# Spreading maxima by one transpose, and casting high halves on GpSimd, in a packed attention + MLP kernel

## The chip, the cores and the metric

One core of a Trainium2 chip runs the whole program. The metric is device time in microseconds (us) per execution.

## The reference

Inputs: `q`, `k`, `v` of 8 batches x 8 heads x 576 positions x 64, `p` of 8 x 8 x 32 x 64, `w_in` 512 x 2048, `w_out` 2048 x 512 (the kernel handles weights of 8-byte floats).

```python
p_packed = sm_attn(p, k, v)             # 32 packed positions attend to k, v
out = sm_attn(q, p_packed, p_packed)    # every q attends to the 32
x = out.transpose(0, 2, 1, 3).reshape(B * S, H * D)
h = x @ w_in
sp = maximum(h, 0) + log1p(exp(-abs(h)))
return (h * erf(sp)) @ w_out
```

## The kernel before, in words

For each batch b the packed result p_packed is folded into `w_in` (`w_prime`), so that h = a2 @ w', where a2 are the second softmax's weights. Products are made in parts: a high part plus a low remainder. Batches 0 and 1 use fp32r parts; batches 2 to 7 use 16-bit (f16) parts, which need scales that are powers of two, so that nothing leaves f16's range.

The work is cut into 128 **units** (b, c, i): a half c of a batch's 576 positions and a pair i of 128-blocks of d_ff. A unit is 12 matmuls of h (`h_half`, two halves of 6, L598), the gate on ScalarE and VectorE, a split into `gh` and `gl`, and 24 matmuls of o (`o_part`, four parts d, L650), which come some steps later. Units 0 to 31 are batches 0 and 1; their activations are softplus and erf. From unit 32 a form with tanh is used.

The first 20 units stand in an order written out by hand (`BEGINNING`). After them `step(n, outs)` issues unit n's h, then the o parts of earlier units, and between these what the table `plan` holds for `(n, where)`: `do(n, 0)` and `do(n, 1)` behind the first o part, `do(n, 3)` behind the third, `do(n, 2)` at the step's end. `ATTEND` (batches 2 and 3) and `ATTEND_LATER` say in which slots the generator `attention(b)` makes its next piece. Every engine executes in the order of issue; `keep_order` fixes it.

PSUM: `ps_h` has two banks, taken in turn by the halves of h, by single-bank scores and by the small products below; `ps_m` is one tile of two banks, used by `w_prime`, by scores and by the attention's tile `p`; `ps_o` holds the four o sums. SBUF: the ring `wo` (18 tiles) holds the parts of `w_out`, the reloaded pairs `wox` and their halves `woh`.

**The scales.** `tallest_in` and `tallest_out` (L175) take per-partition maxima of `w_in` and `w_out`; `gather` (L195) reduces them to one column. `turn` (L201) transposes this column to one row in a `ps_h` bank, and `two_over` (L187 to L190, three VectorE instructions) makes 2/max of it as one number. `spread` (L209, L211) multiplies that number by a row of ones, which puts it on all 128 partitions, in another `ps_h` bank, and copies it to SBUF. The norm of each batch from 2 on goes the same way: L498 transposes, `two_over` reduces, and `spread_norm` (L219, L221) spreads; here both rows and columns lie in spare columns of the `ps_m` tile `p`, which stays taken until the copy L221.

`out_weights` makes `sigma` from the maximum of `w_out`; `whole(i)` reloads a pair of `w_out`'s blocks from DRAM (SP queue), and `halve(i)` makes the f16 high half on ScalarE (L254) and the low half on VectorE (L255), for i = 0 to 7, in steps 30 to 37:

```python
both = opool.tile([P, 2, 2, DM], F16, name=f"woh{i}", tag="wo")
nc.scalar.mul(both[:, 0], pairs[i][:], sigma[:])
nc.vector.scalar_tensor_tensor(both[:, 1], pairs[i][:], sigma[:], both[:, 0], ...)
```

GpSimd (POOL) makes memsets at the start and issues the output DMAs of batches 0 and 1 (L665, L667).

Of the kernel before, what the change touches and what calls it, by code (L numbers as in the profile page):

```python
# [8 lines left out]
F32 = mybir.dt.float32  # L9
# [6 lines left out]
ALU = mybir.AluOpType  # L16
# [25 lines left out]
K12 S12 W1.3 W1.2 o11.0 o10.1 o11.1 o10.3 h15.0 H1.3 L14 F15 s14 V1.3 H1.2 T12 h15.1 L13 o11.3 p11.1 m12 U12 d15.1 M0 C  # L42
o10.2 o11.2 v12 c15.0 s15 h16.0 p11.2 p11.0 h16.1 c16.1 K14 m13 R14 o12.2 d16.0 s16 K13 S13 u13 v13 p11.3 e14 T13
o12.1 h17.0 h19.0 d19.0 o12.0 m14 e15 V1.2 m15 o12.3 e16 U14 v14 L15 K15 h17.1 c17.1 o13.1 o13.0 h19.1 c17.0 C c19.1
S15 o13.3 o14.1 h18.0 h18.1 m16 O0 O1 s19 s17 d18.0 C C C d18.1 M1 M2 M3 s18 e18 U15 o14.0 m18 e19 v15 e17 o13.2 o14.2 T15 m19 o14.3
# [5 lines left out]
def tile_pack_attention_moe(ctx: ExitStack, tc: tile.TileContext, qT, kT, v, pT, w_in, w_out, outT):  # L51
    nc = tc.nc
    P = 128
    B, _, NC, S = qT.shape
# [37 lines left out]
    ones = cpool.tile([1, P], F32, name="ones")  # L92
# [15 lines left out]
    nc.gpsimd.memset(ones[:], 1.0)  # L108
# [89 lines left out]
    def turn(kind):  # L198

        row = ps_h.tile([P, 512], F32, name=f"row_{kind}", tag="ps_h")  # L200
        nc.tensor.transpose(row[0:1, 0:P], halved[kind][:], ident[:])  # L201
        one = cpool.tile([1, 1], F32, name=f"one_{kind}")
        two_over(one[:], row[0:1, 0:P])
        halved[kind] = one

    def spread(kind):

        row = ps_h.tile([P, 512], F32, name=f"col_{kind}", tag="ps_h")
        nc.tensor.matmul(row[:, 0:1], ones[:], halved[kind][:], start=True, stop=True)  # L209
        inverse[kind] = cpool.tile([P, 1], F32, name=f"inv_{kind}")  # L210
        nc.vector.tensor_copy(inverse[kind][:], row[:, 0:1])  # L211
# [4 lines left out]

    def spread_norm(b, po, one):

        nc.tensor.matmul(po[:, 2 * P:2 * P + 1], ones[:], one[:], start=True, stop=True)  # L219
        inverse[b] = apool.tile([P, 1], F32, name=f"inv{b}", tag="inv")  # L220
        nc.vector.tensor_copy(inverse[b][:], po[:, 2 * P:2 * P + 1])  # L221
# [29 lines left out]
    def halve(i):  # L251

        both = opool.tile([P, 2, 2, DM], F16, name=f"woh{i}", tag="wo")
        nc.scalar.mul(both[:, 0], pairs[i][:], sigma[:])  # L254
        nc.vector.scalar_tensor_tensor(both[:, 1], pairs[i][:], sigma[:], both[:, 0], op0=ALU.mult, op1=ALU.subtract)  # L255
        for k in range(2):
            half_hi[2 * i + k], half_lo[2 * i + k] = both[:, 0, k, :], both[:, 1, k, :]
# [23 lines left out]
    ATTEND_LATER = ((-12, 2), (-6, 0), (-6, 1), (-4, 0), (-4, 1), (-4, 2), (-3, 2), (-2, 3), (-2, 2), (-1, 3), (-1, 2),  # L281
                    (0, 0), (0, 1), (1, 0), (1, 1), (1, 2), (2, 0), (2, 1), (4, 0), (4, 1),
# [44 lines left out]
    def attention(b):  # L327
# [169 lines left out]
        if b >= NB0:  # L497
            nc.tensor.transpose(po[0:1, P:2 * P], norm[:], ident[:])  # L498
# [4 lines left out]
        if b >= NB0:  # L503
            one = apool.tile([1, 1], F32, name=f"one{b}", tag="one")
            two_over(one[:], po[0:1, P:2 * P])
            if not third:
                yield
                spread_norm(b, po, one)
        yield
        ta = apool.tile([P, 2, S], F32, name=f"ta{b}", tag="big", bufs=3)  # L510
        for c2 in range(2):
            banks = bank(f"s2_{c2}", b > NB0 + 1 or (b >= NB0 and c2 == 0) or (b == 1 and c2 == 1))
            for c in range(NC):
                for r in range(2):
# [270 lines left out]
    def slot(n, where):  # L785
        return plan.setdefault((n, where), [])
# [123 lines left out]
```

## Time and profile before

| | |
|---|---|
| time, median of 3 (lowest to highest) | 706.14 us (705.68 to 707.76) |
| the profiled execution | 706.21 us, of which the span is 704.4 us |
| PE busy | 682.3 us, 97% |
| VectorE (DVE) busy | 596.9 us, 85% |
| ScalarE (ACT) busy | 563.1 us, 80% |
| GpSimd (POOL) busy | 44.8 us, 6%, all of it in the first third |
| granted TensorE clock | 0.999 of 2.4 GHz |

Time outside the span (1.8 us) belongs to the start and end of the execution. A line like "PE wp L551 <- DVE inv L221: 2.5, 4, 0.7" says that PE's instructions of line 551 waited 2.5 us in all, 4 times, for VectorE's line 221. In a timeline, the bracket behind an instruction is the idle time before it and what ended it.

### The profile page before, as it was taken

Reading aid. Unit: us, or ns where it says so; the run is one execution under the profiler, and the core shown is the slowest. Engines: PE = TensorE matmul, PEld = TensorE weight load, DVE = VectorE, ACT = ScalarE, POOL = GpSimd, SP = SyncE. Lnnn points to the kernel's source line nnn. Section 1 sums busy time; section 2 is a strip of 40 time slices with the busy share of each in tenths; the row PEclk is TensorE's granted clock in tenths of the full one; section 3 lists DMA queues with packets and bytes.
Section 4 is the critical chain, followed back from the end, with each engine's and each line's share of the span. In section 5 each row is a group of like instructions: output and inputs, shape, how many; then the busy total and the mean of one; then the engine's idle time right before and its main releaser. Section 6 shows DMA issues by size and latency. Waiting matters only on the chain.

```text
span 704.4 us, 15671 instructions
## 1 busy us (share of the span) xinstructions
PE 682.3 (97%) x6458; PEld 539.4 (77%) x6458; DVE 596.9 (85%) x945; ACT 563.1 (80%) x987; POOL 44.8 (6%) x75
## 2 busy tenths in 40 slices
PE   8899999999899899999999999999999999999997
PEld 6687989988798577867777676777777677777775
DVE  4999998989687999879988899788988799887775
ACT  3799879957778879888888888978798888888784
POOL 2031122111122000000000000000000000000000
PEclk9999999999999999999999999999999999999999
DMA  9986556275332322111122201132021101000010
GB/s 316 407 316 213 158 176 225 89 264 165 64 63 21 98 64 94 50 71 64 34 60 86 99 1 34 55 113 71 1 89 46 41 1 35 1 9 27 2 34 34
DMA packets 34311, 66.81 MB, mean 95 GB/s; under 512 B 4032, under 2 KB 13248, under 8 KB 34240
## 3 DMA queue, kind: packets, MB, share of 16 engines
q1 hardware_dynamic: 29600, 56.31, 23.6%
q0 software_dynamic: 4352, 8.92, 5.2%
q8 instruction: 50, 0.82, 0.5%
q10 hardware_dynamic: 288, 0.59, 0.2%
q14 instruction: 21, 0.17, 0.1%
HBM read 49.81 MB, written 15.99 MB: 93 GB/s over the span
## 4 chain that ended last, share of the span: by engine, by line
PE 44%; DVE 26%; ACT 22%; issue 4%; DMA 2%; POOL 1%; ACTq 0%; DVEq 0%; POOLq 0%
PE o L650 25%; PE h L598 13%; DVE t L683 6%; DVE t L684 6%; ACT t L681 4%; ACT t L679 4%; DVE gl L633 4%; ACT u L682 3%; ACT t L686 3%; PE wp L551 3%; DVE gh L626 2%; DVE hs L688 2%; ACT ob L662 1%; ACT hs L608 1%; PE s L515 1%
## 5 line engine op out<-in xcount | busy, mean ns | idle before, releaser
L650 PE MATMUL o<-gh,woh 128*128 128x288 f16 x1536 | 304.5, 286 | 1.8 <-ACT ob L660 0.9
L650 PEld LDWEIGHTS <-woh 128*128 128x128 f16 x2304 | 223.4, 98 | 68.4 <-issue 12.8
L650 PE MATMUL o<-gl,woh 128*128 128x288 f16 x768 | 219.6, 286 | 0.5 <-DVE gl L633 0.4
L598 PE MATMUL h<-a2h,wph 128*128 128x288 f16 (+1 forms) x512 | 148.9, 291 | 1.9 <-ACT hs L608 0.7
L598 PE MATMUL h<-a2h,wpl 128*128 128x288 f16 (+1 forms) x512 | 147.7, 289 | 1.2 <-DVE wpl L575 1.2
L598 PE MATMUL h<-a2l,wph 128*128 128x288 f16 (+1 forms) x512 | 147.5, 288 | 0.0
L683 DVE SCALAR_TENSOR_TENSOR t<-hs,gs,t 128x576 f32<-128x576 f32 x96 | 78.2, 814 | 49.6 <-ACT u L682 49.0
L686 ACT ACTIVATE t<-t 128x576 f32<-128x576 f32 x96 | 65.8, 685 | 42.5 <-DVE t L684 41.1
L633 DVE TENSOR_TENSOR gl<-hs,gh 128x576 f16<-128x576 f32 (+1 forms) x124 | 93.9, 758 | 5.9 <-ACT gh L626 1.9
L650 PE MATMUL o<-gh,wohl 128*128 128x288 f32 x448 | 98.3, 300 | 0.0
L608 ACT ACTIVATE hs<-h 128x288 f32<-128x288 f32 x192 | 71.8, 408 | 32.2 <-PE h L598 30.2
L598 PEld LDWEIGHTS <-wph 128*128 128x128 f16 x768 | 74.4, 98 | 20.4 <-issue 1.6
L650 PEld LDWEIGHTS o<-gh,wohl 128*128 128x128 f32 x448 | 74.3, 188 | 5.5 <-issue 1.8
L684 DVE SCALAR_TENSOR_TENSOR t<-u,t 128x576 f32<-128x576 f32 x96 | 72.7, 758 | 3.3
L688 DVE SCALAR_TENSOR_TENSOR hs<-t,hs 128x576 f32<-128x576 f32 x96 | 71.9, 749 | 3.8 <-ACT t L686 3.8
L679 ACT ACTIVATE t<-hs,gs 128x576 f32<-128x576 f32 x96 | 73.8, 769 | 0.0
L681 ACT ACTIVATE t<-t 128x576 f32<-128x576 f32 x96 | 65.6, 683 | 3.0
L682 ACT ACTIVATE u<-t 128x576 f32<-128x576 f32 x96 | 65.6, 683 | 3.1
L650 PE MATMUL o<-gl,wohl 128*128 128x288 f32 x224 | 66.3, 296 | 0.4 <-DVE gl L633 0.4
L626 DVE CAST gh<-hs 128x576 f16<-128x576 f32 (+1 forms) x117 | 53.1, 454 | 6.7 <-PE o L650 6.4
L598 PEld LDWEIGHTS <-wpl 128*128 128x128 f16 x384 | 37.6, 98 | 9.5
L650 PEld LDWEIGHTS o<-gl,wohl 128*128 128x128 f32 x224 | 42.2, 188 | 0.7 <-DVE gl L633 0.6
(134 smaller groups left out, 828.3 us busy)
## 6 DMA issues: line engine op xcount, KB each, us to landing
q<-qT SPq DMA_DIRECT2D x32, 288.0 KB, 4.2
k<-kT SPq DMA_DIRECT2D x30, 288.0 KB, 4.8
wos<-w_out SPq DMA_DIRECT2D x16, 512.0 KB, 5.7
outT<-ob SPq DMA_DIRECT2D x48, 144.0 KB, 1.8
v<-v SPq DMA_DIRECT2D x24, 256.0 KB, 4.3
wi<-w_in SPq DMA_DIRECT2D x12, 512.0 KB, 6.5
outT<-ob POOLq DMA_DIRECT2D x32, 144.0 KB, 3.3
scratch<-wo POOLq DMA_DIRECT2D x16, 256.0 KB, 2.7
```

Source lines behind the costliest of these rows:

```text
L598: nc.tensor.matmul(ps[:, 0:HT], w[:, r, fo:fo + P], a[:, r, c * HT:(c + 1) * HT], start=(m == 0), stop=(m == 5))
L608: nc.scalar.mul(dst, src, 2.0 ** -19)
L626: copy(ghi[:], gs[n][0][:])
L633: nc.vector.tensor_tensor(glo[:], hs[:], ghi[:], op=ALU.subtract)
L650: nc.tensor.matmul(acc[b, c, d][:, 0:HT], w[f][:, d * P:(d + 1) * P], gg[:, k, :], start=(first and k == 0 and m == 0), stop=(last and k = ...
L679: nc.scalar.activation(t[:], hs[:], AF.Tanh, bias=T_BIAS, scale=scale[:, 0:1])
L681: nc.scalar.activation(t[:], t[:], AF.Square, bias=root * Q_BIAS, scale=root * Q_SCALE)
L682: nc.scalar.activation(u[:], t[:], AF.Tanh, bias=U_BIAS, scale=U_SCALE / A2)
L683: nc.vector.scalar_tensor_tensor(t[:], hs[:], scale[:, 1:2], t[:], op0=ALU.mult, op1=ALU.add)
L684: nc.vector.scalar_tensor_tensor(t[:], u[:], A1, t[:], op0=ALU.mult, op1=ALU.add)
L686: nc.scalar.activation(t[:], t[:], AF.Tanh, bias=A_BIAS, scale=A_SCALE)
L688: nc.vector.scalar_tensor_tensor(hs[:], t[:], 1.0, hs[:], op0=ALU.add, op1=ALU.mult)
```

## The change

1. `turn` and the norm's transpose no longer transpose a column into one row. The column is read as 128 equal columns (`to_broadcast`), so the transpose puts the whole row of maxima on every partition, and `two_over` leaves its result on all 128 partitions at once. `spread`, `spread_norm`, the row of ones and the copies L211 and L221 are gone, and with them one piece of `attention(b)`.
2. `halve` is split. `halve_high` is made by GpSimd (`tensor_scalar` with two multiplications, the second by 1), `halve_low` stays on VectorE.
3. `gather` and `turn` of both maxima, `out_weights`, `whole`, and the halves move up by one to three steps; the maxima are taken one earlier each.

```diff
     def turn(kind):
         row = ps_h.tile([P, 512], F32, name=f"row_{kind}", tag="ps_h")
-        nc.tensor.transpose(row[0:1, 0:P], halved[kind][:], ident[:])
-        one = cpool.tile([1, 1], F32, name=f"one_{kind}")
-        two_over(one[:], row[0:1, 0:P])
-        halved[kind] = one
+        nc.tensor.transpose(row[:, 0:P], halved[kind][:].to_broadcast([P, P]), ident[:])
+        inverse[kind] = cpool.tile([P, 1], F32, name=f"inv_{kind}")
+        two_over(inverse[kind][:], row[:, 0:P])
...
-    def halve(i):
+    def halve_high(i):
         both = opool.tile([P, 2, 2, DM], F16, name=f"woh{i}", tag="wo")
-        nc.scalar.mul(both[:, 0], pairs[i][:], sigma[:])
+        nc.gpsimd.tensor_scalar(both[:, 0], pairs[i][:], sigma[:], 1.0, op0=ALU.mult, op1=ALU.mult)
+        halved[i] = both
+
+    def halve_low(i):
+        both = halved[i]
         nc.vector.scalar_tensor_tensor(both[:, 1], pairs[i][:], sigma[:], both[:, 0], op0=ALU.mult, op1=ALU.subtract)
...
         if b >= NB0:
-            nc.tensor.transpose(po[0:1, P:2 * P], norm[:], ident[:])
+            nc.tensor.transpose(po[:, P:2 * P], norm[:].to_broadcast([P, P]), ident[:])
...
         if b >= NB0:
-            one = apool.tile([1, 1], F32, name=f"one{b}", tag="one")
-            two_over(one[:], po[0:1, P:2 * P])
-            if not third:
-                yield
-                spread_norm(b, po, one)
+            inverse[b] = apool.tile([P, 1], F32, name=f"inv{b}", tag="inv")
+            two_over(inverse[b][:], po[:, P:2 * P])
...
-            if third and c2 == 0:
-                spread_norm(b, po, one)
...
-    for k in range(4, 2 * NC):
-        slot(19 + k // 2, 1).append((tallest_in, k))
+    for n, k in ((21, 5), (21, 6), (22, 7)):
+        slot(n, 1).append((tallest_in, k))
     f = 2
-    for n, count in ((22, 4), (23, 1), (24, 2), (25, 3), (26, 1), (27, 2), (28, 1)):
+    for n, count in ((22, 5), (23, 1), (24, 2), (25, 3), (26, 1), (27, 2)):
...
-    for n, where, part, kind in ((22, 1, gather, "in"), (23, 1, turn, "in"), (24, 1, spread, "in"),
-                                 (28, 1, gather, "out"), (29, 1, turn, "out"), (30, 0, spread, "out")):
-        slot(n, where).append((part, kind))
+    for n, kind in ((22, "in"), (27, "out")):
+        slot(n, 1).append((gather, kind))
+        slot(n, 2).append((turn, kind))
...
-    slot(30, 0).append((out_weights,))
+    slot(27, 2).append((out_weights,))
...
-    for i in range(NBLK):
-        slot(24 + i // 2, 1).append((whole, i))
-        slot(30 + i, 3 if i == 0 else 1).append((halve, i))
+    for i, high, low in ((0, 28, 29), (1, 28, 30), (2, 29, 30), (3, 30, 31), (4, 31, 32), (5, 32, 33), (6, 34, 35), (7, 36, 37)):
+        slot(22 + i // 2, 1).append((whole, i))
+        slot(high, 0).append((halve_high, i))
+        slot(low, 1).append((halve_low, i))
```

The queues show three places. **PE in a later batch**, between the last o matmul of a step and the next unit's h (`woh` are the weights of o, `wph` and `wpl` those of h, `p` is the attention's `ps_m` tile). Before:

```order
L650 LDWEIGHTS woh_3059
L650 MATMUL o_1_0_3_3572<-gh_1_6_3825,woh_3059 128x288
L219 MATMUL p_3841<-one_3991,ones 128x1
L598 LDWEIGHTS wph_1_3656
L598 MATMUL h_0_2_0_4028<-a2h_3248,wph_1_3656 128x288
```

Of the change:

```order
L634 LDWEIGHTS woh_2856
L634 MATMUL o_1_0_3_3556<-gh_1_6_3809,woh_2856 128x288
L582 LDWEIGHTS wph_1_3640
L582 MATMUL h_0_2_0_4009<-a2h_3232,wph_1_3640 128x288
```

The product that spread the norm is gone; nothing stands in its place.

**PE at step 28**, behind the last o of step 27, with the semaphores that an instruction waits for. `row_out` is the transposed maxima of `w_out`, `h_1_4_0` and `h_1_4_1` are the two halves of unit 28's h. Of the change (before, no row stands here):

```order
L634 MATMUL o_1_4_3_2186<-gh_1_6_2193,wohl_1500 128x288
L199 MATMUL row_out<-ident,top_out 128x128 [waits DVE_49,Activation_49]
L582 MATMUL h_1_4_0_2358<-a2h_801,wph_2_1405 128x288 [waits Activation_49]
L582 MATMUL h_1_4_0_2358<-a2l_802,wph_2_1405 128x288
L582 MATMUL h_1_4_0_2358<-a2h_801,wpl_2_1406 128x288
L582 MATMUL h_1_4_0_2358<-a2h_801,wph_2_1405 128x288
L582 MATMUL h_1_4_0_2358<-a2l_802,wph_2_1405 128x288
L582 MATMUL h_1_4_0_2358<-a2h_801,wpl_2_1406 128x288
L582 MATMUL h_1_4_1_2366<-a2h_801,wph_2_1405 128x288 [waits Activation_49]
```

The row keeps one of the two `ps_h` banks, so the second half of h is now written to the bank of the first and waits for ScalarE's copy of it. `row_in` does the same at step 23.

**POOL from step 28 on**. Before, outputs of batches 0 and 1 alone:

```order
L665 DMA outT<-ob_1_7_1_2391 128x288
L665 DMA outT<-ob_1_7_2_2400 128x288
L665 DMA outT<-ob_1_7_3_2409 128x288
L665 DMA outT<-ob_0_7_0_2655 128x288
L665 DMA outT<-ob_0_7_1_2676 128x288
```

Of the change, with the semaphores:

```order
L649 DMA outT<-ob_1_7_1_2395 128x288 [waits DMASW5_49,Activation_49]
L238 TENSOR_SCALAR woh_2383<-wox_1882,sigma 128x1024 [waits DMAHW6_49,DVE_49,PE_49]
L238 TENSOR_SCALAR woh_2385<-wox_1884,sigma 128x1024 [waits DMAHW7_49,PE_49]
L649 DMA outT<-ob_1_7_2_2404 128x288 [waits DMASW6_49,Activation_49]
L649 DMA outT<-ob_1_7_3_2413 128x288 [waits DMASW7_49,Activation_49]
L238 TENSOR_SCALAR woh_2450<-wox_1993,sigma 128x1024 [waits DMAHW0_49,DVE_49]
L238 TENSOR_SCALAR woh_2524<-wox_1995,sigma 128x1024 [waits DMAHW1_49,DVE_49]
L238 TENSOR_SCALAR woh_2581<-wox_2081,sigma 128x1024 [waits DMAHW2_49,DVE_49]
L238 TENSOR_SCALAR woh_2662<-wox_2083,sigma 128x1024 [waits DMAHW3_49,DVE_49]
L649 DMA outT<-ob_0_7_0_2650 128x288 [waits DMASW0_49,Activation_49]
```

Each cast from the third on takes the ring buffer of an earlier `wox`, so it waits for VectorE's low half two casts before (`DVE_49`).

## Rows read from the trace of the kernel before

**Rows 1.** Busy time by stage; columns: us, then each engine's busy us (instructions).

```profile
170.00:200.00 30.00, 27.82 (x249) 24.90 (x248) 21.96 (x34) 21.42 (x37) 3.50 (x4) 1.00 0.29 55
200.00:225.00 25.00, 23.90 (x190) 21.21 (x188) 18.20 (x26) 19.75 (x35) 4.40 (x5) 1.00 0.27 30
225.00:248.00 23.00, 19.45 (x247) 14.55 (x246) 20.88 (x38) 18.49 (x33) 2.67 (x3) 1.00 0.42 96
330.00:412.00 82.00, 80.94 (x800) 60.59 (x798) 71.58 (x112) 67.94 (x122) 0.00 (x0) 1.00 0.18 60
```

**Rows 2.** What PE waited for in the whole run: us, times, longest.

```profile
PE wp L551 <- DVE inv L221: 2.5, 4, 0.7
...
PE s L515 <- DVE inv L221: 1.4, 2, 1.1
...
PE p L219 <- DVE one L190: 1.1, 1, 1.1
PE p L422 <- ACT a1t L474: 1.1, 1, 1.1
PE o L650 <- ACT ob L660: 0.9, 1, 0.9
```

**Rows 3.** PE's timeline in batch 5: start, duration, engine, line, operation.

```profile
384.37 0.29 PE L650 MATMUL o<-gl,woh 128*128 128x288 f16 x1
384.49 0.29 PE L650 MATMUL o<-gh,woh 128*128 128x288 f16 x1
384.70 0.38 PE L219 MATMUL p<-one,ones 1*128 1x1 f32 x2
385.01 0.30 PE L598 MATMUL h<-a2h,wph 128*128 128x288 f16 x1
...
388.07 0.66 PE L551 MATMUL wp<-w_in_sb,pt 64*32 64x512 f32 x8 [0.68 <-DVE inv L221]
```

**Rows 4.** PE's timeline in step 24: batch 2's norm and w_in's maximum.

```profile
154.11 0.38 PE L219 MATMUL p<-one,ones 1*128 1x1 f32 x2
154.74 0.72 PE L515 MATMUL s<-q,pt 64*32 64x288 f32 x16 [0.25 <-DVE inv L221]
155.39 0.38 PE L209 MATMUL col_in<-one_in,ones 1*128 1x1 f32 x2
155.70 0.40 PE L650 MATMUL o<-gh,wohl 128*128 128x288 f32 x1
```

**Rows 5.** PE's timeline in steps 29 and 30: w_out's maximum.

```profile
184.27 0.27 PE L201 MATMUL row_out<-ident,top_out 128*1 128x128 f32 x1 [1.54 <-ACT hs L606]
...
191.44 0.38 PE L209 MATMUL col_out<-one_out,ones 1*128 1x1 f32 x2 [0.64 <-ACT a L357]
191.75 0.40 PE L650 MATMUL o<-gh,wohl 128*128 128x288 f32 x1
```

**Rows 6.** ACT's timeline in step 28: the copies of the two halves of h.

```profile
176.43 0.40 ACT L606 COPY hs<-h 128x288 f32<-128x288 f32 x1 [1.01 <-PE h L598]
177.22 0.40 ACT L606 COPY hs<-h 128x288 f32<-128x288 f32 x1 [0.39 <-PE h L598]
```

**Rows 7.** ACT's timeline at 221 us: a high half and the copies behind it.

```profile
221.63 1.15 ACT L254 ACTIVATE woh<-wox,sigma 128x1024 f16<-128x1024 f32 x1
...
224.79 0.98 ACT L660 COPY ob<-o 128x288 f32<-128x288 f32 x3
```

**Rows 8.** Groups of instructions by line and shape: busy us, mean ns, idle before.

```profile
L496 PEld LDWEIGHTS p<-ident,a 128*128 128x128 f32 x8 | 1.1, 140 | 0.8 <-DVE a L487 0.6
...
masks.py:199 POOL TENSOR_SCALAR_AFFINE_SELECT ident<-ident 128x128 f32<-128x128 f32 x1 | 0.3, 282 | 0.0
```

**Rows 9.** Tile view of wo on POOL: ns min/median/max, first and last start.

```profile
L154 POOL MEMSET wo<- x16: 514/526/546, 4.9 to 118.1; 128x512 f32 x16
```

**Rows 10.** Tile view of wox, the reloaded pairs, on the SP queue.

```profile
L249 SPq DMA_DIRECT2D wox<-scratch x8: 360/382/908, 145.6 to 154.9; - x8
```

**Rows 11.** DVE's timeline in the hand-written beginning, behind a maximum of w_in.

```profile
111.17 0.76 DVE L633 TENSOR_TENSOR gl<-hs,gh 128x576 fp32r<-128x576 f32 x1 [1.92 <-ACT gh L626]
```

More of the change, by code (lines that the diff above doesn't have):

```diff
@@ L41 @@
 o8.3 e11 m11 F10 S9 o9.2 h14.1 L12 L10 K10 U10 v10 T9 o9.3 S10 T10 c14.1 c14.0 U11 F14 v11 e13 o10.0 e12 K11 S11 T11
-K12 S12 W1.3 W1.2 o11.0 o10.1 o11.1 o10.3 h15.0 H1.3 L14 F15 s14 V1.3 H1.2 T12 h15.1 L13 o11.3 p11.1 m12 U12 d15.1 M0 C
+K12 S12 W1.3 W1.2 o11.0 o10.1 o11.1 o10.3 h15.0 H1.3 L14 F15 s14 V1.3 H1.2 T12 h15.1 L13 o11.3 p11.1 m12 U12 d15.1 M0 M1 C
 o10.2 o11.2 v12 c15.0 s15 h16.0 p11.2 p11.0 h16.1 c16.1 K14 m13 R14 o12.2 d16.0 s16 K13 S13 u13 v13 p11.3 e14 T13
 o12.1 h17.0 h19.0 d19.0 o12.0 m14 e15 V1.2 m15 o12.3 e16 U14 v14 L15 K15 h17.1 c17.1 o13.1 o13.0 h19.1 c17.0 C c19.1
-S15 o13.3 o14.1 h18.0 h18.1 m16 O0 O1 s19 s17 d18.0 C C C d18.1 M1 M2 M3 s18 e18 U15 o14.0 m18 e19 v15 e17 o13.2 o14.2 T15 m19 o14.3
+S15 o13.3 o14.1 h18.0 h18.1 m16 O0 O1 s19 s17 d18.0 C C C d18.1 M2 M3 M4 s18 e18 U15 o14.0 m18 e19 v15 e17 o13.2 o14.2 T15 m19 o14.3
 m17 T14
@@ L91, in tile_pack_attention_moe @@
     consts = cpool.tile([P, 2], F32, name="consts")
-    ones = cpool.tile([1, P], F32, name="ones")
     w_in_sb = cpool.tile([P, 4, DFF], F32, name="w_in_sb")
@@ L107, in tile_pack_attention_moe @@
         nc.gpsimd.memset(consts[:, i:i + 1], c)
-    nc.gpsimd.memset(ones[:], 1.0)
     def staging(name, n):
@@ L200, in turn @@
         row = ps_h.tile([P, 512], F32, name=f"row_{kind}", tag="ps_h")
-        nc.tensor.transpose(row[0:1, 0:P], halved[kind][:], ident[:])
-        one = cpool.tile([1, 1], F32, name=f"one_{kind}")
-        two_over(one[:], row[0:1, 0:P])
-        halved[kind] = one
-    def spread(kind):
-        row = ps_h.tile([P, 512], F32, name=f"col_{kind}", tag="ps_h")
-        nc.tensor.matmul(row[:, 0:1], ones[:], halved[kind][:], start=True, stop=True)
+        nc.tensor.transpose(row[:, 0:P], halved[kind][:].to_broadcast([P, P]), ident[:])
         inverse[kind] = cpool.tile([P, 1], F32, name=f"inv_{kind}")
-        nc.vector.tensor_copy(inverse[kind][:], row[:, 0:1])
+        two_over(inverse[kind][:], row[:, 0:P])
     def other_way(dst, src):
         nc.vector.tensor_scalar(dst.bitcast(U32), src.bitcast(U32), EXPONENT, None, op0=ALU.bitwise_xor)
[L217 to L221, printed above, removed]
     def scales(b):
@@ L278, in tile_pack_attention_moe @@
         3: ((25, 2), (27, 0), (27, 1), (30, 0), (30, 1), (31, 2), (32, 2), (34, 3), (34, 2), (35, 3), (35, 2),
[1 row of a table removed]
[1 row of a table added]
             (38, 2), (39, 2), (40, 2), (40, 2), (41, 2), (41, 2), (42, 2), (43, 2), (43, 2))}
     ATTEND_LATER = ((-12, 2), (-6, 0), (-6, 1), (-4, 0), (-4, 1), (-4, 2), (-3, 2), (-2, 3), (-2, 2), (-1, 3), (-1, 2),
-                    (0, 0), (0, 1), (1, 0), (1, 1), (1, 2), (2, 0), (2, 1), (4, 0), (4, 1),
+                    (0, 0), (0, 1), (1, 0), (1, 1), (2, 0), (2, 1), (4, 0), (4, 1),
                     (5, 2), (6, 2), (7, 2), (7, 2), (8, 2), (8, 2), (9, 2), (10, 2), (10, 2))
```

2 rows, old and new, of the table ATTEND are left out of this document.

## The prediction

> **What bounds the kernel now.** I read the profile in three steps. First, the busy time by stage [rows 1]. From 248 us on PE is at work without a gap worth the name: one whole batch, 330 to 412, has PE at 80.94 of 82.00 us, and DVE (71.58) and ACT (67.94) have room beside it. There a microsecond off PE's queue is a microsecond off the end. The stage 225 to 248 is another matter: PE 19.45 of 23, so it waits 3.55 us, with DVE at 20.88 and ACT at 18.49. The stages 170 to 200 and 200 to 225 lie between, with 2.2 and 1.1 us of PE idle.
>
> Second, what PE waited for [rows 2]. The longest sums name what this change touches: `w_prime` waits 2.5 us, four times, for the copy of a spread norm (L221), since that copy frees the bank of `p`; the second scores of batch 3 wait 1.1 us for the same line; the spreading product itself waits 1.1 us for `two_over`. Two more, for `a1t` (1.1) and for `ob` (0.9), name copies on ACT. Third, the timeline around these waits [rows 3 to 7], to see what stands ahead of each.
>
> **The change part by part.** The sum is made against the profiled execution, 706.21 us (span 704.4); the median of the runs, 706.14, is the same within 0.1.
>
> *The norm in batches 4 to 7.* In batch 5 the last o matmul starts at 384.49 and the next h at 385.01, 0.52 us later, where one matmul follows another after 0.12 (384.37 to 384.49) [rows 3]. So the spreading product costs 0.40 us of PE, four times 1.6. Then `w_prime` waits 0.68 us [rows 3]; the four such waits sum to 2.5 [rows 2]. In the change `two_over` itself writes all partitions and is the last reader of `p`. It stands where it stood in DVE's order, ahead of the product at 384.70, while the wait ended at 388.07 [rows 3]; so the bank is free some 3 us before `w_prime` comes. Both go: 4.1 us. The order shows nothing in their place. What is late next there: nothing that I find, DVE has 10 us per batch to spare.
>
> *Stage 200 to 248, batch 3's norm and the high halves.* Gone with the spread: the wait of the product (1.1), the product (0.4 as above), and the wait of the scores (1.1) [rows 2]. The other two waits stand behind a high half on ACT: the cast takes 1.15 us at 221.63, and the `ob` copies that PE waits for come at 224.79, four instructions later [rows 7]. Without it they come 1.15 us earlier, and the wait was 0.9; the wait for `a1t` (1.1) has the same build. Sum 4.6. This is the term with the least cover: DVE has only 2.1 us idle in the last 23 [rows 1], and PE running 4.6 us faster asks it to work closer together. For it speaks that the low halves move up: of the five that are now made in steps 33 to 37 three remain.
>
> *w_out's maximum, steps 28 to 30.* `row_out` waits 1.54 us for a `ps_h` bank; `col_out` waits 0.64 and takes 0.31 (191.44 to 191.75) [rows 5]. All this goes, 2.5 us. Added is a new wait: the row takes a bank between two steps, so the second half of unit 28's h waits until ACT has copied the first. That copy takes 0.40, [rows 6], and the draining of the first half ahead of it some 0.2 (a matmul's record lasts 0.29, and the next one starts after 0.12 [rows 3]): 0.6 us. ACT waited for PE at both copies, so nothing else delays it. Net gain 1.9.
>
> *w_in's maximum and batch 2's norm, steps 23 and 24.* The product L219 and the wait behind it go, 154.11 to 154.74, and `col_in`, 155.39 to 155.70 [rows 4]: 0.94. The same new bank wait at step 23 costs 0.6. Net gain 0.3.
>
> *The wide transposes.* Eight column loads become loads of 128 columns, 140 ns each [rows 8], so at most 1.1 us; they run beside matmuls, and I take 0.3 of loss.
>
> *GpSimd's casts.* No such instruction is in the trace. Bounds per cast of 128x1024: a memset of 128x512 takes 526 ns [rows 9], twice that is 1.05 us, and it reads nothing; the only POOL row that reads and writes takes 282 ns for 128 columns [rows 8], eight times that is 2.26 us, too much since its start is counted eight times. I take 1.7, nearer to the row that reads. Eight are 14 us, over steps 28 to 36, on an engine that does little else. Each is issued a step ahead of the low half that needs it, so on the path I cost them at nothing; their cover is that step, some 7 us (176.43 lies in step 28 [rows 6], 191.44 in step 30 [rows 5]). The output DMAs queued behind them on POOL are late by two casts at most; their buffers are wanted again only when the next half batch is put out.
>
> Does a cast slow DVE down? The row: the sixteen memsets take 514 to 546 ns whatever DVE does [rows 9]. They only write, so this does not settle it. By it the term of 4.6 stands. The Trainium skill, "GPSIMD Engine Reference", section 8 (Key points), says that GpSimd shares its SBUF interfaces with VectorE and contends with instructions in a 2-port mode or with two SBUF inputs. No row here shows such a meeting; by that rule the sum would be the first rival's.
>
> *What moves at no cost.* One maximum of `w_in` goes into the hand-written beginning, where DVE sits idle 1.92 us behind another [rows 11]. Four `wox` loads pass batch 3's `p` and two `k` loads on the SP queue: at most 4 times 0.9 us [rows 10], with some 20 us until those are read. If that cover is gone, batch 3's first scores wait. The cast from the third on waits for the low half two before it; that is ready a step ahead.
>
> Sum: 4.1 + 4.6 + 1.9 + 0.3 - 0.3 = 10.6. **706.2 - 10.6 = 695.6 us.** Between the bounds (the stage of 4.6 giving back half; the two bank waits of 0.6 being absorbed by waits that are there anyway, and ACT's 9 us of freed time shortening others) its own range is 692.5 to 698.
>
> **The rivals.**
>
> 1. *The casts contend with DVE.* GpSimd works 14 us while DVE has 8.0 us idle in 170 to 200 and 6.8 in 200 to 225 [rows 1]. If DVE's two-input instructions stand still for half of that, 7 us, the idle time takes some and the rest makes `gl` late, in the stage where DVE is already full. Price: the 4.6 us of that stage are not gained. Time 695.6 + 4.6 = 700.2. For it: nearly all DVE work there has two SBUF inputs. By the skill's rule above this is the likelier case. Against: most casts fall before 215 us, where DVE has room.
>
> 2. *A wait changes places only.* PE's queue in 170 to 248 is bound by the chain ACT to DVE to PE, not by the spread; then the waits of these stages come back under other names (`ob`, `a1t`, `hs`) and `w_prime` waits for another reader of `p`. Gained are only the products, 1.6 + 0.4 + 0.3, less 0.3: 704.2. Against: the order shows no other late reader, and ACT is relieved.
>
> 3. *Slower: the cast is slow.* DVE's low halves wait in order, with `gh` and `gl` behind them, and PE behind these. From `sigma` in step 28 (about 178, just behind [rows 6]) to the low halves 1 and 2 in step 30 (about 191 [rows 5]) POOL must do three casts and two DMA issues of 0.88 (3.50 for 4 [rows 1]): it decides from (13 - 1.8) / 3 = 3.7 us per cast. Past 6.5 us, a step's length, each of four more casts in the following steps is late too. At 8 us: 3 x 8 + 1.8 - 13 = 12.8, and 4 x 1.5 = 6: 695.6 + 18.8 = 714.4. It takes some 7 us, three times the upper bound, to lose the whole gain. For it: a pointer scalar, two multiplications and f16 output, none of which a POOL row shows.
>
> **How the numbers follow.** Forecast 0.66, rival 1 0.22, rival 2 0.05, rival 3 0.07. A change of under 0.3% (2.1 us) can't be told from none in this kernel. Forecast and rival 1 are faster: 0.88; rival 2, at -2.0, counts as no change: 0.05; rival 3 is slower: 0.07. The range takes in the forecast and nearly all of rival 1, 692 to 701.5; outside are rivals 2 and 3 and some 0.06 of tails.
>
> **What would show it.** In the profile after: no L551 or L515 wait for `inv`; batches of 81.0 us instead of 82.0 (each loses 0.40 + 0.68); a PE wait of about 0.6 at the second half of units 23 and 28, for `hs`; POOL rows of 1.0 to 2.3 us for `woh`; PE's idle time in 225 to 248 down from 3.55 to about 1. If the batches keep 82 us, the spread was not what bound them. If DVE's `gl` grows beyond 0.76 us on average while POOL casts, rival 1 is at work; if DVE waits on POOL, rival 3.

## The result, and the profile after

The changed kernel took 695.65 us (median of four runs, 695.53 to 696.29) beside 706.95 (705.68 to 707.93) of the kernel before in the same comparison: a ratio of 0.984, 95% interval 0.982 to 0.986. The profiled execution took 696.29 us, its span 694.5, at a granted clock of 1.00. PE is busy for 98% of it.

Where the 9.9 us of span came from shows best when the program is cut at the first h matmul of a few units, in the two timelines of PE:

| stretch | before, us | after, us | gain | forecast |
|---|---|---|---|---|
| start to unit 16 | 109.87 | 110.18 | -0.31 | none |
| unit 16 to 25 (w_in, batch 2's norm) | 48.31 | 47.49 | 0.82 | 0.3 |
| unit 25 to 32 (w_out's maximum) | 40.85 | 39.04 | 1.81 | 1.9 |
| unit 32 to 35 | 22.88 | 24.82 | **-1.94** | none |
| unit 35 to 39 (batch 3's norm, queue of ACT) | 26.09 | 21.09 | 5.00 | 4.6 |
| unit 39 to the end (batches 4 to 7) | 456.40 | 451.88 | 4.52 | 4.1 |

The wide transposes, forecast at -0.3, lie inside these rows, and the forecast's 4.6 was for the whole stage 200 to 248; its four waits all lay from 225.2 us on. The rows add up to 9.9 us where 10.6 was forecast, but one stretch lost what no term foresaw. In the two profiles of the changed kernel (the second is after_again below) each unit from 16 on took the same time within 0.03 us. Unit 18 is less steady: it took 4.8 us before and after, but up to 6.6 in other profiles, though no edit touches it. The gain of the second row doesn't hang on it: 0.77 us of it lie in units 22 to 24. The busy time by stage, after, in the stages and columns of [rows 1]:

```profile
170.00:200.00 30.00, 29.50 (x269) 25.50 (x267) 28.22 (x35) 20.24 (x36) 12.30 (x11) 1.00 0.28 55
200.00:225.00 25.00, 23.05 (x180) 20.90 (x173) 19.25 (x25) 16.42 (x32) 8.56 (x9) 1.00 0.27 30
225.00:248.00 23.00, 22.95 (x280) 17.85 (x279) 22.27 (x40) 17.78 (x34) 1.85 (x3) 1.00 0.52 134
330.00:412.00 82.00, 81.62 (x808) 61.32 (x806) 72.73 (x112) 68.95 (x124) 0.00 (x0) 1.00 0.18 60
```

PE's idle time in 225 to 248 is gone (3.55 to 0.05 us), in 170 to 200 it fell from 2.2 to 0.5, but in 200 to 225 it rose from 1.1 to 1.95. DVE's busy time in 170 to 200 rose by 6.3 us; two more low halves in that window are 2.6 of that. What PE waited for, after; the waits for `inv` of [rows 2] are gone:

```profile
PE h L582 <- ACT hs L592: 1.7, 4, 1.0
PE h L582 <- ACT hs L590: 1.7, 3, 0.7
...
PE o L634 <- DVE gh L610: 0.5, 1, 0.5
```

The first row's longest wait (1.0) and the last row are new, and both lie in units 32 to 34. The place of batch 5 that stood in [rows 3], after:

```profile
377.99 0.29 PE L634 MATMUL o<-gl,woh 128*128 128x288 f16 x1
378.11 0.29 PE L634 MATMUL o<-gh,woh 128*128 128x288 f16 x1
378.24 0.29 PE L582 MATMUL h<-a2h,wph 128*128 128x288 f16 x1
...
380.53 1.09 PE L535 MATMUL wp<-w_in_sb,pt 64*32 64x512 f32 x16
```

From o to h it is now 0.13 us, and `w_prime` carries no wait. A batch takes 80.85 us instead of 82.02. The wait for a bank that the forecast added is there, at units 23 and 28, and the copy in it is the one named (the second is at 176.65, with 0.49 too):

```profile
146.47 0.29 PE L582 MATMUL h<-a2h,wpl 128*128 128x288 f32 x1
147.24 0.40 PE L582 MATMUL h<-a2h,wph 128*128 128x288 f32 x1 [0.49 <-ACT hs L590]
```

Now the loss. GpSimd's casts in the changed kernel:

```profile
180.80 2.58 POOL L238 TENSOR_SCALAR woh<-wox,sigma 128x1024 f16<-128x1024 f32 x2
...
187.91 1.25 POOL L238 TENSOR_SCALAR woh<-wox,sigma 128x1024 f16<-128x1024 f32 x1 [2.77 <-DVE woh L244]
192.32 3.97 POOL L238 TENSOR_SCALAR woh<-wox,sigma 128x1024 f16<-128x1024 f32 x2 [3.16 <-DVE woh L244]
197.78 1.26 POOL L238 TENSOR_SCALAR woh<-wox,sigma 128x1024 f16<-128x1024 f32 x1 [1.49 <-DVE woh L244]
...
204.46 1.37 POOL L238 TENSOR_SCALAR woh<-wox,sigma 128x1024 f16<-128x1024 f32 x1 [1.59 <-DVE woh L244]
...
206.96 2.60 POOL L238 TENSOR_SCALAR woh<-wox,sigma 128x1024 f16<-128x1024 f32 x1
```

and DVE's timeline beside three of these moments:

```profile
180.92 2.89 DVE L610 CAST gh<-hs 128x576 fp32r<-128x576 f32 x1 [1.15 <-PE o L634]
183.84 0.76 DVE L617 TENSOR_TENSOR gl<-hs,gh 128x576 fp32r<-128x576 f32 x1
...
187.72 0.45 DVE L610 CAST gh<-hs 128x576 fp32r<-128x576 f32 x1
188.21 1.56 DVE L617 TENSOR_TENSOR gl<-hs,gh 128x576 fp32r<-128x576 f32 x1
...
206.84 1.84 DVE L617 TENSOR_TENSOR gl<-hs,gh 128x576 fp32r<-128x576 f32 x1
```

The groups of `gl` and `gh` to fp32r in the whole run (busy us, mean ns), two rows before the change and two after:

```profile
L633 DVE TENSOR_TENSOR gl<-hs,gh 128x576 fp32r<-128x576 f32 x28 | 21.2, 756 | 2.6 <-ACT gh L626 1.9
L626 DVE CAST gh<-hs 128x576 fp32r<-128x576 f32 x21 | 9.6, 455 | 6.5 <-PE o L650 6.4
...
L617 DVE TENSOR_TENSOR gl<-hs,gh 128x576 fp32r<-128x576 f32 x28 | 25.4, 906 | 1.5 <-ACT gh L610 0.8
L610 DVE CAST gh<-hs 128x576 fp32r<-128x576 f32 x21 | 11.9, 569 | 3.8 <-PE o L634 3.7
```

A `gl` that meets a cast takes 1.5 to 1.8 us instead of 0.76; the `gh` that met two casts took 2.89 instead of 0.45. In all DVE is stretched by 28 x 0.150 = 4.2 and 21 x 0.114 = 2.4, some 6.6 us. The brackets of the casts say why they meet: four of them are released by a low half on DVE (L244), and what DVE does next in its order is `gh` and `gl`. The delay arrives at PE through ACT, which waits 3.30 us for a `gl` that still reads the buffer of `hs`:

```profile
206.47 0.71 ACT L592 ACTIVATE hs<-h 128x288 f32<-128x288 f32 x2 [3.30 <-DVE gl L617]
```

and PE stands 1.02 us behind that copy:

```profile
206.93 0.28 PE L582 MATMUL h<-a2h,wph 128*128 128x288 f16 x1 [1.02 <-ACT hs L592]
```

This wait stands at the end of unit 32, which took 10.23 us instead of 9.05; unit 34 took 6.77 instead of 5.97. The two are the whole loss of 1.94.

### The profile page after: what moved, and what is told of

The parts are those of the page before. It is cut to its first block, busy times and chain, and to the rows that moved or that the text cites. A ratio compares the mean times of both kernels' runs of the same rounds, so it can differ in the third digit from the quotient of the medians.

```text
span 694.5 us, 15631 instructions
## 1 busy us (share of the span) xinstructions
PE 679.1 (98%) x6442; PEld 538.0 (77%) x6442; DVE 602.1 (87%) x937; ACT 554.5 (80%) x979; POOL 56.9 (8%) x82
## 4 chain that ended last, share of the span: by engine, by line
PE 53%; DVE 22%; ACT 16%; issue 4%; DMA 2%; POOL 1%; SPq 0%; ACTq 0%; POOLq 0%; DVEq 0%
PE o L634 30%; PE h L582 16%; DVE t L667 4%; DVE t L668 4%; DVE gl L617 3%; ACT t L665 3%; PE wp L535 3%; ACT t L663 3%; ACT u L666 2%; ACT t L670 2%; DVE gh L610 2%; DMA wi<-w_in 2%; ACT ob L646 2%; DVE hs L672 1%; PE p L411 1%
## 5 line engine op out<-in xcount | busy, mean ns | idle before, releaser
L617 DVE TENSOR_TENSOR gl<-hs,gh 128x576 f16<-128x576 f32 (+1 forms) x124 | 98.1, 791 | 4.8 <-ACT gh L610 0.8
L610 DVE CAST gh<-hs 128x576 f16<-128x576 f32 (+1 forms) x117 | 55.5, 474 | 4.0 <-PE o L634 3.7
```

The source lines that it names most:

```text
L610: copy(ghi[:], gs[n][0][:])
L617: nc.vector.tensor_tensor(glo[:], hs[:], ghi[:], op=ALU.subtract)
```

## The experiments

Each kernel ran beside the kernel before on one chip. Rows with the same median of the kernel before come from one comparison, and their times compare directly; other rows compare by what they gain on the kernel before. The last column is of the profiled execution: from the first h matmul of unit 16 to the end, since the start of the program alone moved by 2.5 us between executions (unit 16 began at 109.2 to 111.7 us). Unit 18 still adds up to 1.8 us of its own to this column, most in norms_4_to_7 and low_after_gl.

| kernel | median, us | before, us | ratio (95%) | unit 16 to end |
|---|---|---|---|---|
| before | | | | 594.5 |
| after | 695.65 | 706.95 | 0.984 (0.982 to 0.986) | 584.3 |
| norms_4_to_7 | 701.61 | 705.88 | 0.994 (0.993 to 0.996) | 591.8 |
| spread_only | 699.58 | 705.88 | 0.992 (0.991 to 0.994) | 588.2 |
| high_on_act | 702.42 | 705.88 | 0.9945 (0.993 to 0.996) | 588.5 |
| high_memset | 694.69 | 705.88 | 0.984 (0.983 to 0.986) | 583.0 |
| after_again | 695.88 | 705.86 | 0.986 (0.984 to 0.988) | 584.3 |
| row_beside_h | 696.24 | 705.86 | 0.987 (0.985 to 0.988) | 584.7 |
| high_on_dve | 697.93 | 705.86 | 0.989 (0.987 to 0.991) | 586.6 |
| low_behind_split | 694.71 | 705.86 | 0.984 (0.982 to 0.986) | 583.2 |
| low_after_gl | 694.87 | 705.87 | 0.984 (0.982 to 0.985) | 584.5 |
| extra_casts | 699.23 | 705.87 | 0.991 (0.989 to 0.993) | 587.2 |
| gl_as_stt | 697.14 | 706.75 | 0.986 (0.984 to 0.988) | 584.6 |
| all_three | 696.67 | 706.75 | 0.985 (0.983 to 0.987) | 583.4 |

**The norms alone.** The kernel before, with this in `attention`, and one step fewer in the table of later batches:

```diff
+            if b > NB0 + 1:
+                nc.tensor.transpose(po[:, P:2 * P], norm[:].to_broadcast([P, P]), ident[:])
...
+        if b > NB0 + 1:
+            inverse[b] = apool.tile([P, 1], F32, name=f"inv{b}", tag="inv")
+            two_over(inverse[b][:], po[:, P:2 * P])
```

> The kernel before, with the spread by transpose in the norms of batches 4 to 7 alone. By the sum: 4 x (0.40 + 0.68, less a trace for the wider load) = 4.1 us less, 702 us, a batch period of 81.0 us instead of 82.0, no wait of w_prime for inv. Rival (the wait changes places: another reader of p holds the bank): only the four products go, 704.5 us, and w_prime waits about 0.6 us each time under another name.

The median fell by 4.3 us. From unit 39 to the end it took 451.90 us: 4.50 less than before, and as long as in the whole change (451.88). Nothing else of the change acts there.

**All spreads, the rest as before.** `turn` and the norms as in the change, `turn` at the end of steps 23 and 29, the maxima, low halves and ACT's casts in their old steps.

> The kernel before, with every spread by transpose and w_out's maximum in its old steps, the high halves on ACT as they were. By the sum: 4.1 (batches 4 to 7) + 2.6 (batch 3: product 0.4 and two waits of 1.1) + 1.9 + 0.3 - 0.3 = 8.6 us less, 697.5 us; the PE waits for ob (0.9) and a1t (1.1) behind a high half on ACT stay. Rival (GpSimd's casts took away as much as they gave): this kernel is as fast as the changed one, 695.6 us, or faster.

It gained 6.3 us, not 8.6 and far from 10. Two places fall short. Units 25 to 32 took 40.28 us, a gain of 0.57 where the change has 1.81, since the row at the end of step 29 holds a bank and unit 30 has to wait:

```profile
187.17 0.29 PE L577 MATMUL h<-a2h,wpl 128*128 128x288 f32 x1
189.37 0.40 PE L577 MATMUL h<-a2h,wph 128*128 128x288 f32 x1 [1.90 <-ACT hs L585]
```

Moving the maximum two steps up is thus worth 1.2 us of its own. And units 35 to 39 took 24.27 us, against 21.09 in the change: without the waits for `inv`, the scores wait 0.77 us for a copy on ACT. The rest of the change (the casts off ACT, the low halves moved) is worth 3.2 us there, more than the 2.0 in the sum; the rival that GpSimd takes as much as it gives falls.

**The high halves back on ACT, in the change's steps.**

```diff
-        nc.gpsimd.tensor_scalar(both[:, 0], pairs[i][:], sigma[:], 1.0, op0=ALU.mult, op1=ALU.mult)
+        nc.scalar.mul(both[:, 0], pairs[i][:], sigma[:])
```

> The changed kernel with its eight high halves on ACT, in the same steps as GpSimd has them. By the sum: the two waits behind ACT's cast come back, 2.0 us, 697.6 us. Theory of contention (gl and gh stretched beside a cast cost PE about 1.5 us at 206.9 and 216.9): these two waits go at the same time, gl and gh are back at 0.76 and 0.455 us on average, and the sum of both is about 696.2 us. Rival (contention costs more than ACT's queue): under 695.

A miss: 702.4, 3.5 us below the kernel before, where all three theories had 694 to 698. (The profiled execution was the fastest of the five, 700.12.) `gl` and `gh` were back and units 32 to 35 took 22.50 us (24.82 in the change), so contention does go. Of the two waits that were to come back, the one for `ob` did (0.94 us, at 226.76), the one for `a1t` didn't. But in steps 28 to 31 the cast waits on ACT for a low half, with the copies of h queued behind it:

```profile
188.21 1.15 ACT L238 ACTIVATE woh<-wox,sigma 128x1024 f16<-128x1024 f32 x1 [1.63 <-DVE woh L244]
...
192.30 0.68 ACT L590 COPY hs<-h 128x288 f32<-128x288 f32 x2
```

```profile
186.33 0.41 PE L582 MATMUL h<-a2h,wph 128*128 128x288 f32 x1 [1.10 <-ACT hs L590]
...
192.74 0.43 PE L382 MATMUL s<-k,p 64*32 64x288 f32 x1 [2.75 <-ACT hs L590]
```

The earlier steps are only open to an engine on which waiting blocks nobody. GpSimd waits as well (9.0 us in four), and no wait of PE names it.

**A memset in place of the cast.** The high halves of w_out are left out.

```diff
-        nc.gpsimd.tensor_scalar(both[:, 0], pairs[i][:], sigma[:], 1.0, op0=ALU.mult, op1=ALU.mult)
+        nc.gpsimd.memset(both[:, 0], 0.0)
```

> The changed kernel with a GpSimd memset of the same 128x2x512 f16 tile in place of each cast: the high halves of w_out are left out, what waits for them is the same. Theory of contention: a memset reads nothing and stretches nothing, so gl and gh come back to 0.76 and 0.455 us on average, the PE waits at 206.9 (1.0, hs) and 216.9 (0.5, gh) go, and the time falls by 1 to 1.5 us, to 694.3. Rival (the chain ACT to DVE to PE of this stage holds PE whatever GpSimd does): the two waits stay and the time is 695.6.

`gl` came back to 756 ns, ACT's copy to 205.00 us, and PE's wait at 206 is gone: unit 33 begins 95.72 us behind unit 16 instead of 96.75. Units 32 to 35 took 23.36 us, 1.46 less than in the change. From unit 16 to the end the profile is 1.3 us shorter; by the medians (11.2 us below the kernel before, the change 11.3 and 10.0 in its two comparisons) the two kernels are not told apart. Two parts of the expectation failed. What waits is not the same: a memset reads neither `sigma` nor `wox`, and the first two ran at 144.71 and 151.57, so the `gh` at 180.92 met nothing. And `gh` stayed at 554 ns on average, and PE's wait for one at 216 only fell from 0.54 to 0.23 us. A memset holds `gh` up as well, though not `gl`:

```profile
187.04 0.76 DVE L617 TENSOR_TENSOR gl<-hs,gh 128x576 fp32r<-128x576 f32 x1
...
202.89 1.28 DVE L610 CAST gh<-hs 128x576 fp32r<-128x576 f32 x1
```

```profile
186.70 1.20 POOL L238 MEMSET woh<- 128x1024 f16 x1 [2.90 <-DVE woh L244]
...
202.91 0.95 POOL L238 MEMSET woh<- 128x1024 f16 x1
```

So what the casts cost beyond such memsets, the first two of which were out of the way, is 1.0 (the wait) to 1.5 us (units 32 to 35), not 4.6. With no instruction of GpSimd there at all, in high_on_act, units 32 to 35 took 2.3 us less than in the change; there PE had lost time in steps 28 to 31, which gave DVE room, so this is taken as an upper bound. The rest of the stretch fell into idle time: in units 29 to 32 DVE is idle for 0.4 us in the change and for 4.0 us here.

**The changed kernel again**, for the next three:

> The changed kernel once more, beside the next three on the same chip: 0.984 of the kernel before, 695 to 696 us. It is what they are compared with.

It came out at 695.88 us, a ratio of 0.986. The last four kernels had no changed kernel beside them.

**The rows in columns that nobody uses.** `row = spare[0][:, HT:HT + P]`, `spare[0]` being the bank taken last.

> The changed kernel with the two wide rows of the maxima put into the unused columns 288 to 415 of the bank that was taken last, so that they take no bank of their own. By the forecast each new bank wait costs PE about 0.6 us (the gaps at 147.2 and 176.7 are 0.64 and 0.66): 1.2 us less than the changed kernel, and no hs wait there. Rival (the second half of h would wait there anyway, for two_over or for ACT): no gain.

No gain, and the wait stands as it was (0.49 behind ACT's copy, at 147.44). DVE reads the row at 150.38, behind `gh`, `gl` and the gate, so that bank is held until then whether the row has it alone or not. What has to move is the reading, not the row.

**The high halves on DVE,** each at the slot of its low half, by `nc.vector.tensor_scalar`.

> The changed kernel with the high halves on DVE, each just ahead of its low half. Estimate of one from the CAST of 576 columns in 0.45 us: 0.8 us, eight are 6.4 us, about as much as GpSimd's casts stretch gh and gl in all (6.6 us). Theory (what counts is the sum on DVE's queue): as fast as the changed kernel within 1 us, gl back at 0.76 us. Rival (0.8 us right ahead of gh in eight steps is worse than a stretch that falls partly into idle time): 1.5 to 3 us slower than the changed kernel.

The rival: 2.0 us slower than the change. A cast took 0.746 us, eight 6.0, and `gl` to fp32r was back at 756 ns. PE waits where one stands ahead of `gh`:

```profile
215.32 0.75 DVE L238 TENSOR_SCALAR woh<-wox,sigma 128x1024 f16<-128x1024 f32 x1
216.11 1.28 DVE L244 SCALAR_TENSOR_TENSOR woh<-wox,sigma,woh 128x1024 f16<-128x1024 f32 x1
217.31 0.45 DVE L610 CAST gh<-hs 128x576 fp32r<-128x576 f32 x1
```

```profile
217.81 0.40 PE L634 MATMUL o<-gh,wohl 128*128 128x288 f32 x1 [1.32 <-DVE gh L610]
```

GpSimd's stretch of 6.6 us is no less work for DVE than this, but it costs PE less, as much of it falls into idle time.

**The low halves earlier.** `slot(low - 1, 2)` in place of `slot(low, 1)`.

> The changed kernel with each low half at the end of the step before, behind gh and gl, instead of ahead of them. A cast on GpSimd is released by a low half on DVE (two before it), so now it runs beside whatever DVE does next, which is gh and gl. Theory (DVE and GpSimd take turns, one whole instruction at a time, when both hold the port): gh and gl come back towards 0.45 and 0.76 us, the two-input instructions behind them (L604, L313) are stretched instead, PE's wait at 206.9 falls by 0.5 us or more, and the time by 0.5 to 1.2 us. Rival (only DVE's sum counts, since it is busy without a pause from 184 to 208 us): the same time as the changed kernel.

Time as expected (694.71 beside 695.88, though the single runs overlap; in the profiles 1.1 us less from unit 16 on), by another cause. In steps below 32 the new slot has the same place in DVE's order, so the low halves 0 to 4 didn't move, `gl` stayed at 0.91 and the wait at 206.9 stayed at 1.01. What moved are the halves 5 to 7. In the change, half 5 stands right ahead of a `gh` that PE waits for:

```profile
215.24 1.28 DVE L244 SCALAR_TENSOR_TENSOR woh<-wox,sigma,woh 128x1024 f16<-128x1024 f32 x1
216.44 0.45 DVE L610 CAST gh<-hs 128x576 fp32r<-128x576 f32 x1
...
216.95 0.40 PE L634 MATMUL o<-gh,wohl 128*128 128x288 f32 x1 [0.54 <-DVE gh L610]
```

Here it falls into idle time at 213, and the waits for `gh` and `gl` are gone: unit 34 takes 5.57 us instead of 6.76. That is more than the 0.80 that unit 34 had lost. The place of half 5 is not the whole cause: in high_on_act it stands in the same place, and unit 34 took 5.59 us without a wait for `gh`. There ACT's copy, with which the chain to this `gh` begins, came 1.6 us ahead of unit 33, in the change only 0.5. So the late half and the casts' delay cost this time together.

**The low halves behind gl.** `slot(low, 2)` for 0 to 4, 5 to 7 as in the last kernel.

> The kernel of low_behind_split with the low halves 0 to 4 really behind gh and gl in DVE's order (there they kept their place, since a step below 32 has no DVE work between its start and that slot; only the low halves 5 to 7 moved). A cast of GpSimd is released by a low half; here gh and gl of that step are done by then. Theory of turns: the casts from the third on meet neither gh nor gl, gl falls from 0.91 to about 0.78 us on average, gh from 0.57 to under 0.50 (the first two casts still meet gh), PE's wait at 206.9 (1.0, hs L592) is gone or under 0.3, and the time is about 1 us below low_behind_split, 693.7 us. Rival (DVE's sum counts, the stretch moves to other instructions): gl back at 0.76 but others longer, the wait at 206.9 stays at 0.7 or more, the time the same.

The rival, mostly. The cast at 190.5 met neither, and two `gl` were back at 0.76; but the later casts came in pairs and met the `gl` at 197.6, 205.1 and 207.1 and a gate; the mean only fell to 0.89 and PE's wait stayed at 1.04. The time is that of low_behind_split (694.87 and 694.71; from unit 25 to the end the profiles differ by 0.2 us). Moving a cast changes whom it meets; DVE is as late at 205 us.

**More casts in the steady batches.**

```diff
+        tile = apool.tile([P, 2 * DM], F16, name=f"extra{n}", tag="extra", bufs=1)
+        nc.vector.tensor_copy(tile[:, 0:1], sigma[:])
+        nc.gpsimd.tensor_scalar(tile[:], w_in_sb[:, 0, 0:2 * DM], sigma[:], 1.0, op0=ALU.mult, op1=ALU.mult)
...
```

> The changed kernel with sixteen more casts of 128x1024 on GpSimd in the steady batches (about 375 to 470 us), each released by a DVE copy of one column, in odd units just ahead of gh, in even units just behind gl. Their results are not used. Theory of turns: gh (SBUF to SBUF, 0.45) and gl (two SBUF inputs, 0.76) and the scalar_tensor_tensor with two SBUF inputs each wait out the rest of a cast that began before them, so the one that follows is longer by up to 1.2 us; transposes from PSUM, and instructions with a PSUM input, are not. The batch has some 10 us of DVE to spare, 8 casts cost it 8 x 1 = 8 us, so the time grows by less than 2 us. Rival (only gh and gl to fp32r are touched, not f16): no DVE mean there changes. Rival (each cast costs PE its length): 16 us slower.

DVE and GpSimd beside each other, a scalar_tensor_tensor, a reduction and a `gl`:

```profile
392.60 0.75 DVE L678 SCALAR_TENSOR_TENSOR hs<-t,hs 128x576 f32<-128x576 f32 x1
...
402.80 1.34 DVE L295 TENSOR_REDUCE mx<-ta 128x36 f32<-128x1152 f32 x1
...
406.31 0.45 DVE L616 CAST gh<-hs 128x576 f16<-128x576 f32 x1
406.79 1.55 DVE L623 TENSOR_TENSOR gl<-hs,gh 128x576 f16<-128x576 f32 x1
```

```profile
392.78 1.54 POOL L245 TENSOR_SCALAR extra<-w_in_sb,sigma 128x1024 f16<-128x1024 f32 x1 [165.34 <-DVE extra L244]
...
402.98 1.12 POOL L245 TENSOR_SCALAR extra<-w_in_sb,sigma 128x1024 f16<-128x1024 f32 x1 [5.65 <-DVE extra L244]
406.49 1.25 POOL L245 TENSOR_SCALAR extra<-w_in_sb,sigma 128x1024 f16<-128x1024 f32 x1 [2.39 <-DVE extra L244]
```

The eight `gl` behind a cast took 1.55 us each, to f16 as to fp32r. The scalar_tensor_tensor kept its 0.75, and the cast took 1.54; beside the reduction both kept their times. The price was higher than expected, 3.3 us by the medians (each against its kernel before) and 2.9 in the profile: the batch took 83.70 us instead of 80.84. `gl` is stretched by 8 x 0.79 = 6.3 us and the copies add 16 x 0.15 = 2.4, less than the 10 us that DVE has to spare. But the loss lies in three units alone, 74, 75 and 78 (0.70, 1.12 and 1.03 us), where PE's new waits name ACT; in the other thirteen the stretch cost nothing. Why these three, no run shows.

**gl by scalar_tensor_tensor.** The last rows left two readings: this instruction is spared, or it was spared because it began first.

```diff
+            nc.vector.scalar_tensor_tensor(glo[:], hs[:], 1.0, ghi[:], op0=ALU.mult, op1=ALU.subtract)
```

> The changed kernel with the low half gl of the units below 32 made by scalar_tensor_tensor, (hs x 1.0) - gh, instead of tensor_tensor; the extra casts stretched every tensor_tensor that met one from 0.76 to 1.55 us and left scalar_tensor_tensor with two SBUF inputs at 0.75. Theory (the kind of instruction decides which has to wait): gl to fp32r falls from 0.91 to 0.76 us on average beside the same casts, which grow instead; DVE is 1.5 us earlier at 199 us, PE's wait of 1.0 at 206.9 is under 0.2, and the time is 1.0 to 1.5 us below the changed kernel, 694.6. Rival (two inputs in SBUF decide, the extra casts met scalar_tensor_tensor by another order): gl stays near 0.9 and the time the same, 695.8.

The theory fell. The gain on the kernel before is 9.6 us, no more than the change's, `gl` stays at 906 ns, and the first that begins behind a cast reads as before, beside a cast at 187.41 of 1.26 us:

```profile
187.71 1.55 DVE L618 SCALAR_TENSOR_TENSOR gl<-hs,gh 128x576 fp32r<-128x576 f32 x1
```

So it is not the choice between these two instructions that decides, and of the two readings the order of beginning is left.

**All edits together.**

> gl_as_stt with two edits more: the low halves 5 to 7 half a step earlier, as in low_behind_split (which took 1.1 us from the waits at 216), and the wide rows one o part earlier in their step, so that DVE reads them ahead of gh and gl and their bank is free for the second half of the next unit (one maximum of w_out goes from step 27 to 26, so that the row needn't wait for it). Sum: 1.0 to 1.5 + 1.1 + 2 x 0.65 = 3.4 to 3.9 us below the changed kernel, 692.2 us, with no hs wait at 147 and 177. Rival (the bank is taken by another tile in its place, or the row waits for its maximum): 1.3 less of it, 693.5.

As the last kernel had gained nothing, 1.0 to 1.5 us of this sum were lost already; the gain of the earlier low halves is there (unit 34: 5.59 us, no wait for `gh`). The wait at unit 23 went, worth 0.23 us (unit 23 took 5.60 instead of 5.83): DVE now read the row at 146.85. The wait at unit 28 went and another came, as the rival had it, because DVE had not finished the maximum:

```profile
176.55 0.29 PE L199 MATMUL row_out<-ident,top_out 128*128 128x128 f32 x1 [0.80 <-DVE top_out L193]
```

From unit 16 on it takes 583.4 us, no better than low_behind_split. By the medians no version that does the whole work is shown to be faster than the change: low_behind_split gained 11.2 us on the kernel before and low_after_gl 11.0, the change 11.3 and 10.0. Only the shorter unit 34 in the profiles, 5.6 to 5.8 us instead of 6.8, speaks for the earlier low halves. The wait at 206.9 went only where GpSimd made no cast: in high_memset, which leaves the work out, and in high_on_act, which pays for it elsewhere; in high_on_dve it was 0.66.

## Why the prediction was right, and where it was not

The time, 695.6 forecast (692 to 701.5) and 695.65 measured, and the mechanisms of four terms stand (the profiled execution, against which the sum was made, came out 9.9 us lower, not 10.6; the medians fell by 11.3 us in one comparison and 10.0 in the other, so an agreement to 0.05 us is luck). That it is so close is partly two errors that cancel: the gains came out at 12.1 us (0.82 + 1.81 + 5.00 + 4.52) where 10.6 was forecast, and 1.9 was lost where the forecast had nothing.

- **Batches 4 to 7: right, under-sized.** 4.52 for 4.1. The product took 0.40 as forecast; the step with the wait of `w_prime` got 0.77 us shorter (6.79 to 6.02), not 0.68. The bank is free in time, and nothing took its place (norms_4_to_7 by itself gives the same).
- **Stage 225 to 248: right.** 5.0 for 4.6, all four waits and the product gone, PE idle 0.05 us where about 1 was forecast. spread_only shows the parts: 1.8 by the spread alone, 3.2 by the rest.
- **w_out's maximum: right,** 1.8 for 1.9. Units 29 and 30 gave 2.8 where 2.5 was forecast; the new wait made unit 28 0.84 us longer where 0.6 was forecast, and the row 0.2 in unit 27. In spread_only, where the maximum stays in its old step, only 0.6 is left.
- **w_in's maximum: right in sign,** 0.8 for 0.3. Step 24 gave 1.07 for 0.94; step 23 grew by 0.29, not 0.6, though the wait is there: in the kernel before, this step held the row's own transpose and 0.18 us of idle time.
- **GpSimd's casts: the step that failed.** "on the path I cost them at nothing", and "By it the term of 4.6 stands", resting on memsets that take the same time whatever DVE does. That row told of GpSimd's time, and never of DVE's. The first rival's mechanism is real: DVE is stretched by 6.6 us. Its place and price were wrong: not the stage 225 to 248, where 4.6 us were to be lost, but units 32 to 34, where PE loses 1.0 to 1.5 us by high_memset, and at most 2.3 by high_on_act. The rest fell into DVE's idle time. The size of a cast was right by accident: 1.68 us on average, made of 1.12 alone (extra_casts, 402.98) and of waiting for DVE.
- **The low halves moved up: counted only as a help.** Half 5 now stands ahead of a `gh` that PE waits for, and moving it was worth 1.2 us (low_behind_split). It costs that only while the casts make the chain late (high_on_act), so this and the casts' price overlap; together they are the 1.9.

The rule of the Trainium skill that the prediction weighed ("GPSIMD Engine Reference", section 8, Key points) agrees with the trace in that DVE and GpSimd contend. The time that the prediction drew from it, the first rival's 700.2 us, didn't come; what the contention does to the time had to come from the rows.

## What to carry to other kernels

Work given to an idle engine can be paid for by another one that it contends with, as VectorE paid for GpSimd's casts here: look up which instructions of the busy engine will run beside it, who releases the new work, and what stands next in the releaser's order, because that is what it will meet. Then ask when the busy engine's delay comes due; here 6.6 us of stretch cost PE 1.0 to 2.3, the rest fell into idle time. A change that takes a wait away from a queue is worth measuring part by part, as neighbouring parts hide or uncover one another (with the wide row in place, moving a maximum two steps was worth 1.2 us; without it the move was not tried).

## What was not expected of the hardware

Where they met, DVE and GpSimd took turns by whole instructions, and in most rows whichever began first kept its time. Behind a cast on GpSimd, `gl` with two SBUF inputs takes 1.55 us (0.76 alone) by either instruction, and `gh`, an SBUF-to-SBUF CAST, took 2.89 behind two of them (0.45 alone). If `gh` begins first it keeps 0.45, and a scalar_tensor_tensor that began first kept 0.75 while the cast took 1.54 instead of 1.12. A reduction (1.34) and the `wpl` subtraction with a PSUM input (1.27, at 195.23 in the change) are not touched. A memset on GpSimd, which reads nothing, leaves `gl` at 0.76 but stops `gh` (1.28).

Some rows don't fit so plain an order. The second of the two casts that held `gh` up at 180.92 began at 181.90, 0.99 us behind `gh`, and still went ahead of it; so did the second of two casts around a `gl` in low_after_gl (207.05, 2.92 us). The `gl` at 206.84 began 0.12 us ahead of its cast and took 1.84. The `gh` at 202.89 in high_memset began 0.02 us ahead of the memset and took 1.28. What decides in such cases is not shown.

The Trainium skill, "SBUF — State Buffer", section "Who interferes with whom", says that the shared port pair is an exclusive lock held for the whole instruction, taken by whoever issues first, and that two SBUF inputs on VectorE contend only with a GpSimd instruction that reads SBUF. The rows agree with it but for those of the last paragraph, where no record shows in what order the lock was asked for. That a memset stops `gh`, which has one input, is not a case of the sentence on two inputs.
